# Moving weight loads, ordering the last transfers, spin matmuls and a pipelined MLP in a cached-attention decode kernel

## The chip, the cores and the metric

The kernel runs on one core of one Trainium2 chip. The metric is the device time of one execution in microseconds; the kernel before takes 878.12 us (median of 13 runs, 876.05 to 878.97). Engines are called PE (TensorE), PEld (its weight loads), DVE (VectorE), ACT (ScalarE), POOL (GpSimd) and SP (SyncE, which here only issues DMAs). A profiled execution has a span some 1.8 us shorter than its device time.

## The reference

Two rounds of attention and MLP on a tiny activation (8 rows of 640), with a large cache:

```python
x = x + A(layernorm(x));  x = x + B(layernorm(x))      # and both once more
# A: q = x @ wq (640 x 4096), 32 heads of 128; the last 1024 positions of k_cache, v_cache
#    p = softmax(q k^T / sqrt(128)); o = p v; return o @ wo (4096 x 640)
# B: y = layernorm(x); h = gelu(y @ w1 + b1) (640 x 1728); return h @ w2 + b2
```

Each attention reads 64 MB of K and 64 MB of V in bf16, in 32 chunks of 2 MB each (8 heads of one batch row). Weights: WQ 5.2 MB, WO 5.2 MB, W1 and W2 2.2 MB each.

## The kernel before

Per chunk, DVE makes the scores of 6 heads (48 fused multiply-and-sum instructions), PE those of 2; ACT takes the exps; PE multiplies with V ("PV", 64 one-column matmuls). K has three buffers, V two. K is issued on SP's DMA queue, V on ACT's. WO has no memory of its own: it goes into the K buffers when their last chunk is done.

```python
@block.gpsimd                                  # at the start of the program
def _(g):
    ...
    S_W1.inc(g.dma_start(W1[:, :, :], ...))    # 2.2 MB
    S_W2.inc(g.dma_start(W2[:, 0:FC - 1, :], ...))
    S_W2.inc(g.dma_start(W2[0:F_LAST, FC - 1, :], ...))

@block.scalar
def _(sc):
    S_WQ.inc(sc.dma_start(WQ[:, :, :], ...))   # 5.2 MB; K waits for it
...
# in the attention, on SP, after the last K chunk:
for (c, i, h0, nh) in sorted(woq):             # c: last chunk of K buffer i
    sy.wait_ge(S_QKD.handle, qkd_end[c])       # DVE is done with it
    sy.wait_ge(S_PQ.handle, ...)               # PE is done with it
    S_WO[i].inc(sy.dma_start(WOB[i][:, :, :], A_wo[h0 * Dh:(h0 + nh) * Dh, :]...))
...
# PE at the end of the attention
emit_pv(NCHUNK - 1)                            # waits for exps and for the last V
emit_den(bt0 + B - 1)
...                                            # broadcast of 1/den, OTS on DVE, then
for n0, n1 in [(0, 512), (512, D)]:            # the projection: 32 wide, 32 narrow
    for h in range(H):
        ins = t.matmul(WO_PS[0:8, n0:n1], OTS[:, h * 8:h * 8 + 8], WO(h)[:, n0:n1], ...)
...
# the MLP, each engine by itself over 4 column groups:
#   PE:  W1, all groups      DVE: u, v, z of all groups     ACT: tanh of all groups
#   DVE: h of all groups     PE: transposes, DVE: copies    PE: second projection, all
```

The score loop on DVE, which the change leaves alone, is the line named L347 before and L345 after.

The softmax here doesn't subtract the row's maximum and nothing guards it: scores larger than these inputs give would overflow.

## Time and profile before

| piece of the span (us) | before | what it holds |
|---|---|---|
| start to first score instruction | 35.2 | WQ, first layer norm, first K |
| first score loop | 363.9 | 32 chunks, DVE busy |
| between the loops | 59.6 | last PV, projection, MLP, layer norms, new q |
| second score loop | 364.3 | the same |
| after it | 51.5 | last PV, projection, MLP |
| span | 874.5 | |

The borders are the first and last score instruction of each attention in the timeline. The lines of the profile behind this table stand in the prediction: the chain, the waits of DVE, the chain in order of time and a few stretches. A line of a stretch gives from:to and the length in us, then the busy time and the number of instructions of PE, PEld, DVE, ACT and POOL, then the granted clock (1.00 is full), the DMA share and GB/s. Of the names, KVALL holds the K and V buffers and the WO parts, MPS is the sum of PV, ACC the sum of a projection, OTS what the output projection reads, XT the activation to which a result is added. QROW are the matmuls that make the new q; u, v, z and h are the steps of the MLP's gelu on DVE, hts the copies of its transposes.

### The profile page before, as it was taken

How to read it: one execution, taken by the hardware profiler on the slowest of the kernel's cores; microseconds unless marked ns; L12 is line 12 of the kernel's file. 1: busy time of each engine (PE TensorE's matmuls, PEld its weight loads, DVE VectorE, ACT ScalarE, POOL GpSimd, SP SyncE). 2: the span in 40 equal slices, each digit the busy share in tenths (PEclk: the TensorE clock that was granted, in tenths of full speed). 3: DMA queues.
4: the chain of work that ended last, by engine and by line, in shares of the span. 5: the costliest groups of instructions: out<-in, count | busy, mean ns of one | idle time of the engine just before them, and what ended most of it. 6: DMA issues, size and time to landing. Idle time of an engine off the chain costs nothing.

```text
span 874.5 us, 23472 instructions
## 1 busy us (share of the span) xinstructions
PE 531.3 (61%) x6964; PEld 305.7 (35%) x6964; DVE 732.7 (84%) x6324; ACT 351.8 (40%) x1343; POOL 3.9 (0%) x11
## 2 busy tenths in 40 slices
PE   0866656565666665665458776656565656665456
PEld 0433333333333333342224443333333333333222
DVE  1399999999999999993529999999999999999615
ACT  3444444444434444440335544444444444444121
POOL 1000000000000000000000000000000000000000
PEclk9955555555555555555777555555555555555577
DMA  9999999999999999994706999999999999999800
GB/s 372 381 387 386 385 364 377 365 373 365 372 369 376 379 366 370 368 355 149 288 15 234 359 385 386 386 385 372 370 362 374 360 380 360 378 369 366 282 3 1
DMA packets 143072, 290.16 MB, mean 332 GB/s; under 512 B 2256, under 2 KB 10464, under 8 KB 142304
## 3 DMA queue, kind: packets, MB, share of 16 engines
q1 hardware_dynamic: 74864, 144.72, 45.2%
q10 hardware_dynamic: 67248, 139.50, 43.9%
q0 software_dynamic: 832, 4.44, 1.3%
q8 instruction: 55, 0.90, 0.4%
q14 instruction: 73, 0.60, 0.2%
HBM read 288.64 MB, written 0.01 MB: 330 GB/s over the span
## 4 chain that ended last, share of the span: by engine, by line
DVE 80%; DMA 7%; PE 6%; issue 4%; ACT 2%; DVEq 1%; ACTq 0%
DVE SCRD L347 73%; DVE MLPSCR L347 4%; PE ACC L632 3%; DMA WQ<-in_A_wq_dram 2%; DMA KVALL<-in_A_v_cache_dram 2%; DMA KVALL<-in_A_k_cache_dram 1%; PE ACC L759 1%; DMA KVALL<-in_A_wo_dram 1%; PE P L675 1%; DVE DSUM L318 1%; DVE RDEN L320 1%; DVEq L346 0%; ACT L251 0%; ACT L249 0%; PE MPS L448 0%
## 5 line engine op out<-in xcount | busy, mean ns | idle before, releaser
L347 DVE CUSTOM_DVE_ANT_0 SCRD<-KVALL,QBCB 128x128 bf16<-128x128 bf16 x3072 | 683.6, 287 | 57.9 <-DMA KVALL<-in_A_k_cache_dram 20.9
L347 DVE DVE_READ_ACCUMULATOR2_ANT MLPSCR<- 128x1 f32 x3072 | 250.6, 82 | 0.2
L532 ACT ACTIVATE KTS<-P 128x128 bf16<-128x128 bf16 x512 | 142.1, 278 | 163.8 <-PE P L414 59.0
L520 ACT ACTIVATE QBCB<-P 128x512 bf16<-128x512 f32 x128 | 69.4, 594 | 221.4 <-DVE MLPSCR L347 213.2
L381 PE MATMUL P<-QROWS,UF 8*128 8x512 bf16 x128 | 62.5, 578 | 145.1 <-ACT QBCB L520 143.7
L532 ACT ACTIVATE KTS<-TPS 128x128 bf16<-128x128 bf16 x512 | 139.6, 273 | 2.4
L414 PE MATMUL TPS<-IDENT,KVALL 128*128 128x128 bf16 x512 | 139.9, 273 | 0.0
L414 PE MATMUL P<-IDENT,KVALL 128*128 128x128 bf16 x512 | 138.1, 270 | 0.0
L448 PE MATMUL MPS<-MLPSCR,KVALL 128*128 128x1 bf16 x4096 | 119.2, 165 | 20.3 <-DMA KVALL<-in_A_v_cache_dram 19.4
L424 PE MATMUL P<-QCOL,KTS 128*128 128x1 bf16 x512 | 91.2, 187 | 57.8 <-ACT KTS L532 56.8
L424 PE MATMUL ACC<-QCOL,KTS 128*128 128x1 bf16 x512 | 91.0, 187 | 54.0 <-ACT KTS L532 53.5
L448 PEld LDWEIGHTS MPS<-MLPSCR,KVALL 128*128 128x128 bf16 x4096 | 114.1, 104 | 25.4 <-issue 18.9
L424 PEld LDWEIGHTS P<-QCOL,KTS 128*128 128x128 bf16 x512 | 54.0, 105 | 119.4 <-ACT KTS L532 110.4
L424 PEld LDWEIGHTS ACC<-QCOL,KTS 128*128 128x128 bf16 x512 | 54.0, 105 | 114.6 <-ACT KTS L532 105.2
L381 PEld LDWEIGHTS P<-QROWS,UF 8*128 8x128 bf16 x128 | 12.1, 98 | 172.1 <-issue 149.8
L414 PEld LDWEIGHTS P<-IDENT,KVALL 128*128 128x128 bf16 x512 | 59.4, 116 | 26.9 <-issue 26.9
L414 PEld LDWEIGHTS TPS<-IDENT,KVALL 128*128 128x128 bf16 x512 | 59.8, 117 | 0.0
L367 PE MATMUL P<-WQ,YTS 128*8 128x512 bf16 x80 | 20.8, 422 | 11.0 <-DMA WQ<-in_A_wq_dram 9.6
L632 PE MATMUL ACC<-KVALL,OTS 128*8 128x128 bf16 (+1 forms) x128 | 22.7, 345 | 3.6 <-DMA KVALL<-in_A_wo_dram 2.4
L228 ACT ACTIVATE UF<-XT 8x640 f32<-8x640 f32 x4 | 2.9, 735 | 53.9 <-DVE XT L641 41.3
L551 ACT ACTIVATE MLPSCR<-MLPSCR 128x48 bf16<-128x48 f32 x64 | 15.6, 244 | 16.7 <-DVE MLPSCR L347 16.7
L641 DVE TENSOR_TENSOR XT<-XT,ACC 8x640 f32<-8x640 f32 x2 | 1.6, 808 | 24.0 <-PE ACC L632 24.0
(67 smaller groups left out, 182.7 us busy)
## 6 DMA issues: line engine op xcount, KB each, us to landing
KVALL<-in_A_k_cache_dram SPq DMA_DIRECT2D x64, 2048.0 KB, 17.2
KVALL<-in_A_v_cache_dram ACTq DMA_DIRECT2D x64, 2048.0 KB, 18.2
KVALL<-in_A_wo_dram SPq DMA_DIRECT2D x4, 1920.0 KB, 12.5
WQ<-in_A_wq_dram ACTq DMA_DIRECT2D x1, 5120.0 KB, 21.8
KVALL<-in_A_wo_dram SPq DMA_DIRECT2D x2, 1280.0 KB, 16.4
W<-in_B_w_dram POOLq DMA_DIRECT2D x1, 2160.0 KB, 16.8
W<-in_B_w_dram POOLq DMA_DIRECT2D x1, 2080.0 KB, 23.8
W<-in_B_w_dram POOLq DMA_DIRECT2D x1, 80.0 KB, 23.7
```

The costliest lines, as they stand in the source:

```text
L318: S_DVM.inc(v.tensor_reduce(out=DSUM[:, :], in_=den[0:1, 0:H * J].rearrange("p (h j) -> p h j", j=J), axis=AXX, op=ALU.add))
L320: v.reciprocal(out=RDEN[:, (pb - bt0) * H:(pb - bt0 + 1) * H], in_=DSUM[:, :])
L347: ins = v.tensor_tensor_reduce(out=SCRD[:, slot, :], in0=k_buf[:, hh, j, :], in1=QBCB[gc % 2][:, hh, :], scale=SCALE, scalar=0.0, op0=ALU. ...
L367: ins = t.matmul(QRPS[gq % 2][0:8, 0:QG * Dh], YTS[:, c, :], WQ[:, c, qg * QG * Dh:(qg + 1) * QG * Dh], start=(c == 0), stop=(c == DC - 1))
L381: S_QBM.inc(t.matmul(QPS[qb % 2][:, :], SELB[0:8, b, :], QROWS[0:8, (g * HC + hf * QG) * Dh:(g * HC + (hf + 1) * QG) * Dh], start=True, st ...
L414: S_TP.inc(t.transpose(TPOS[n % 2][:, 0:128], k_buf[:, hh, j, :], IDENT128[:, :]))
L424: S_PQ.inc(t.matmul(SCPS[gc % 2][:, col:col + 1], KTS[n % 2][:, :], QCOL[:, h, b:b + 1], start=True, stop=True))
L448: ins = t.matmul(OTP[:, col:col + 1], v_buf[:, hh, j, :], PB[bt % 2][:, h * J + j:h * J + j + 1], start=(j == 0), stop=(j == J - 1))
L520: S_QEB.inc(sc.activation(QBCB[gc % 2][:, hf * QG:(hf + 1) * QG, :], QPS[qb % 2][:, :].rearrange("p (h d) -> p h d", h=QG), ACTF.Copy))
L532: S_KTE.inc(sc.activation(KTS[n % 2][:, :], TPOS[n % 2][:, 0:128], ACTF.Copy))
L551: S_EXP.inc(sc.activation(PB[bt % 2][:, g * HC * J:(g * HC + hdv) * J], SB[bt % 2][:, g * HC * J:(g * HC + hdv) * J], ACTF.Exp))
L632: ins = t.matmul(WO_PS[0:8, n0:n1], OTS[:, h * 8:h * 8 + 8], WO(h)[:, n0:n1], start=(h == 0), stop=(h == H - 1))
```

## The change

Its intent: use DMA where it idles and keep PE's clock up where DVE does not work. (1) The MLP weights leave the start and follow WO on SP's queue. (2) WO's heads are dealt out in the order in which the K buffers come free, so the projection uses the parts as they arrive (they were already issued in that order), and the second part waits for the last V. (3) "Spin" matmuls, whose results nobody reads, stand before, between and after the real ones. (4) The MLP's four groups are interleaved over the engines. (5) SP issues the first two V chunks of the second attention early.

```diff
-            S_W1.inc(g.dma_start(W1[:, :, :], ...))          # on GpSimd, at the start
-            S_W2.inc(g.dma_start(W2[:, 0:FC - 1, :], ...))
-            S_W2.inc(g.dma_start(W2[0:F_LAST, FC - 1, :], ...))
...
+        def spin(t, dst, n):
+            # matmuls whose result nobody reads: they only keep TensorE's clock up
+            for _ in range(n):
+                t.matmul(dst[0:8, 0:512], IDENT128[:, 0:8], WQ[:, 0, 0:512], start=True, stop=True)
...  # layer norm, all but the first of the program
+                    spin(t, MPS, 10)
+                    t.wait_ge(S_ACM.handle, acm_stat)
+                    spin(t, MPS, 8)
+                    t.wait_ge(S_ACM.handle, acm_sqrt)
+                    spin(t, MPS, 4)
                 t.wait_ge(S_ACM.handle, acm_y)
...                  # transposes of y
+                    spin(t, MPS, 4)
...  # end of the attention, PE
+                t.wait_ge(S_QKD.handle, qkd_end[gc0 + NCHUNK - 1] - 2)
+                spin(t, QPS[0], 9)
                 emit_pv(NCHUNK - 1)
                 emit_den(bt0 + B - 1)
+                spin(t, QPS[0], 3)
...                  # broadcast of 1/den
+                spin(t, QPS[0], 3)
...  # ACT, V loads
+                    if a >= 1 and ci < NVB:
+                        S_VDB[gc % NVB].count += 16
+                        return
...  # SP, K loads
+                    if a >= 1 and ci == NKB - 1:
+                        for ce in range(NVB):
+                            ...                       # V chunk ce of the second attention
...  # SP, WO parts, sorted by their buffer's last chunk
+                    if idx_ == 1:
+                        lastg = gc0 + NCHUNK - 1
+                        sy.wait_ge(S_VDB[lastg % NVB].handle, 16 * (lastg // NVB + 1))
...
                 if a == 0:
+                    S_W1.inc(sy.dma_start(W1[:, :, :], ...))
+                    S_W2.inc(sy.dma_start(W2[:, 0:FC - 1, :], ...))
+                    S_W2.inc(sy.dma_start(W2[0:F_LAST, FC - 1, :], ...))
...  # MLP: after W1 spin(t, MPS, 6), after the first transposes spin(t, MPS, 4), and the order
+            dve_uvz(0); act_tanh(0); dve_uvz(1); act_tanh(1); dve_h(0); pe_T(0)
+            dve_uvz(2); act_tanh(2); dve_hts(0); pe_o2(0); dve_h(1); pe_T(1)
+            dve_uvz(3); act_tanh(3); dve_hts(1); pe_o2(1); dve_h(2); pe_T(2)
+            dve_h(3); pe_T(3); dve_hts(2); pe_o2(2); dve_hts(3); pe_o2(3)
```

(The last four lines are one call per line in the source.) With the new dealing the WO parts also have other sizes: in the first attention the part that goes first has 12 heads instead of 8.

More of the change, by code (lines that the diff above doesn't have):

```diff
@@ L94, in bass_interleave_layers__sliding_block_cached__mixer_channel_mlp__decode_kernel @@
         HPK = KU // D
-        WO_PARTS = []
-        _h0 = 0
-        for _i in range(NKB):
-            _nh = min(HPK, H - _h0)
-            WO_PARTS.append((_i, _h0, _nh))
-            _h0 += _nh
-        assert _h0 == H
-        WOB = [KVALL[:, i * KU:i * KU + nh * D].rearrange("p (k n) -> p k n", k=nh) for (i, h0, nh) in WO_PARTS]
-        def WO(h):
-            for pi, (i, h0, nh) in enumerate(WO_PARTS):
-                if h0 <= h < h0 + nh:
-                    return WOB[pi][:, h - h0, :]
-            raise AssertionError
+        assert HPK * NKB >= H
+        WOB = [KVALL[:, i * KU:i * KU + HPK * D].rearrange("p (k n) -> p k n", k=HPK) for i in range(NKB)]
         QBCB = [T(f"QBCB{i}", [128, HC, Dh], BF16) for i in range(2)]
@@ L204, in _ @@
             S_GD.inc(g.dma_start(XT[0][0:B, :], A_x.rearrange("b s d -> (b s) d")))
-            S_W1.inc(g.dma_start(W1[:, :, :], B_w1.rearrange("(c p) n -> p c n", p=128)))
-            S_W2.inc(g.dma_start(W2[:, 0:FC - 1, :], B_w2[0:(FC - 1) * 128, :].rearrange("(k p) n -> p k n", p=128)))
-            S_W2.inc(g.dma_start(W2[0:F_LAST, FC - 1, :], B_w2[(FC - 1) * 128:F, :]))
         G_SETUP = S_G.count
@@ L220, in bass_interleave_layers__sliding_block_cached__mixer_channel_mlp__decode_kernel, with emit_ln_yt @@
         DVM_IDENT = S_DVM.count
-        def emit_ln_yt(xin, x_ready_waits):
+        def emit_ln_yt(xin, x_ready_waits, warm=False):
             @block.scalar
@@ L267, in _ @@
             def _(t):
+                if warm:
+                    spin(t, MPS, 10)
[3 more added lines that the diff above has]
+                    spin(t, MPS, 4)
                 t.wait_ge(S_ACM.handle, acm_y)
@@ L273, in _ @@
                 S_PEM.inc(ins)
+                if warm:
+                    spin(t, MPS, 4)
             pem_yt = S_PEM.count
@@ L287, in emit_A @@
             a = glob["a"]
-            dvm_yts = emit_ln_yt(xin, x_ready)
+            dvm_yts = emit_ln_yt(xin, x_ready, warm=(a >= 1))
             gc0 = glob["gc"]
@@ L485, in _ @@
                             emit_den(bt0 + (ci - 1) // NG)
+                t.wait_ge(S_QEB.handle, 2 * (gc0 + NCHUNK))
+                t.wait_ge(S_QKD.handle, qkd_end[gc0 + NCHUNK - 1] - 2)
+                spin(t, QPS[0], 9)
                 emit_pv(NCHUNK - 1)
                 emit_den(bt0 + B - 1)
+                spin(t, QPS[0], 3)
                 t.wait_ge(S_RDEN.handle, bt0 + B)
@@ L594, in _ @@
                     assert S_KDB[kbi].count == 16 * (gc // NKB + 1)
-                woq = []
-                for (i, h0, nh) in WO_PARTS:
+                    if a >= 1 and ci == NKB - 1:
+                        for ce in range(NVB):
+                            ge = gc0 + ce
+                            sy.wait_ge(S_PV.handle, ge - NVB + 1)
+                            sy.dma_start(VB[ge % NVB][:, :, :, :], A_v_cache[ce // NG, (ce % NG) * HC:(ce % NG + 1) * HC, W0:W0 + W, :].rearrange("h (p j) d -> p h j d", p=128)).then_inc(S_VDB[ge % NVB].handle, 16)
+                order = sorted(range(NKB), key=lambda i: max(cc for cc in range(gc0, gc0 + NCHUNK) if cc % NKB == i))
+                womap = {}
+                h0 = 0
+                for i in order:
+                    nh = min(HPK, H - h0)
+                    womap[i] = (h0, nh)
+                    h0 += nh
+                assert h0 == H
+                glob["womap"] = womap
+                for idx_, i in enumerate(order):
                     c = max(cc for cc in range(gc0, gc0 + NCHUNK) if cc % NKB == i)
-                    woq.append((c, i, h0, nh))
-                for (c, i, h0, nh) in sorted(woq):
                     sy.wait_ge(S_QKD.handle, qkd_end[c])
                     sy.wait_ge(S_PQ.handle, blk_base[c] + hpe_of(c) * J)
-                    S_WO[i].inc(sy.dma_start(WOB[i][:, :, :], A_wo[h0 * Dh:(h0 + nh) * Dh, :].rearrange("(k p) n -> p k n", p=128)))
+                    if idx_ == 1:
+                        lastg = gc0 + NCHUNK - 1
+                        sy.wait_ge(S_VDB[lastg % NVB].handle, 16 * (lastg // NVB + 1))
+                    hh0, nh = womap[i]
+                    S_WO[i].inc(sy.dma_start(WOB[i][:, 0:nh, :], A_wo[hh0 * Dh:(hh0 + nh) * Dh, :].rearrange("(k p) n -> p k n", p=128)))
                 glob["wo_val"] = [S_WO[i].count for i in range(NKB)]
                 if a == 0:
-                    pass
+                    S_W1.inc(sy.dma_start(W1[:, :, :], B_w1.rearrange("(c p) n -> p c n", p=128)))
+                    S_W2.inc(sy.dma_start(W2[:, 0:FC - 1, :], B_w2[0:(FC - 1) * 128, :].rearrange("(k p) n -> p k n", p=128)))
+                    S_W2.inc(sy.dma_start(W2[0:F_LAST, FC - 1, :], B_w2[(FC - 1) * 128:F, :]))
             @block.vector
@@ L622, in _, with wo_of @@
             def _(t):
+                spin(t, QPS[0], 3)
                 t.wait_ge(S_DVM.handle, dvm_ots)
+                womap = glob["womap"]
+                def wo_of(h):
+                    for i, (hh0, nh) in womap.items():
+                        if hh0 <= h < hh0 + nh:
+                            return i, WOB[i][:, h - hh0, :]
+                    raise AssertionError
                 ins = None
@@ L627, in _ @@
                     for h in range(H):
-                        pi = [k for k, (i, h0, nh) in enumerate(WO_PARTS) if h0 <= h < h0 + nh][0]
+                        pi, wt = wo_of(h)
                         if pi not in waited:
@@ L631, in _ @@
                             waited.add(pi)
-                        ins = t.matmul(WO_PS[0:8, n0:n1], OTS[:, h * 8:h * 8 + 8], WO(h)[:, n0:n1],
+                        ins = t.matmul(WO_PS[0:8, n0:n1], OTS[:, h * 8:h * 8 + 8], wt[:, n0:n1],
                                        start=(h == 0), stop=(h == H - 1))
@@ L651, in emit_B @@
         def emit_B(xin, xout, x_ready):
-            dvm_yts = emit_ln_yt(xin, x_ready)
+            dvm_yts = emit_ln_yt(xin, x_ready, warm=True)
             GCOLS = [(0, 512), (512, 1024), (1024, 1536), (1536, F)]
+            NGRP = len(GCOLS)
             @block.vector
@@ L670, in _, with dve_uvz @@
                     ins = None
-                    n0 = g0
-                    while n0 < g1:
-                        n1 = min(n0 + 512, g1, ((n0 // 512) + 1) * 512)
-                        for c in range(DC):
-                            ins = t.matmul(HP[0:8, n0:n1], YTS[:, c, :], W1[:, c, n0:n1], start=(c == 0), stop=(c == DC - 1))
-                        n0 = n1
+                    for c in range(DC):
+                        ins = t.matmul(HP[0:8, g0:g1], YTS[:, c, :], W1[:, c, g0:g1], start=(c == 0), stop=(c == DC - 1))
                     S_PEM.inc(ins)
                     pem_hp[gi] = S_PEM.count
+                spin(t, MPS, 6)
             dvm_z = {}
-            @block.vector
-            def _(v):
-                v.wait_ge(WA_B[0].handle, WA_B[1])
-                for gi, (g0, g1) in enumerate(GCOLS):
+            acm_t = {}
+            dvm_h = {}
+            pem_ht = {}
+            dvm_hts = {}
+            pem_o2 = {}
+            def dve_uvz(gi):
+                g0, g1 = GCOLS[gi]
+                @block.vector
+                def _(v):
                     v.wait_ge(S_PEM.handle, pem_hp[gi])
-                    if gi > 0:
-                        v.wait_ge(S_DVM.handle, S_DVM.count)
+                    v.wait_ge(WA_B[0].handle, WA_B[1])
+                    v.wait_ge(S_DVM.handle, S_DVM.count)
                     S_DVM.inc(v.tensor_tensor(UB[0:B, g0:g1], HP[0:B, g0:g1], B1[0:B, g0:g1], ALU.add))
@@ L695, in _, with act_tanh @@
                     dvm_z[gi] = S_DVM.count
-            acm_t = {}
-            @block.scalar
-            def _(sc):
-                for gi, (g0, g1) in enumerate(GCOLS):
+            def act_tanh(gi):
+                g0, g1 = GCOLS[gi]
+                @block.scalar
+                def _(sc):
                     sc.wait_ge(S_DVM.handle, dvm_z[gi])
@@ L703, in _, with dve_h @@
                     acm_t[gi] = S_ACM.count
-            dvm_h = {}
-            @block.vector
-            def _(v):
-                for gi, (g0, g1) in enumerate(GCOLS):
+            def dve_h(gi):
+                g0, g1 = GCOLS[gi]
+                @block.vector
+                def _(v):
                     v.wait_ge(S_ACM.handle, acm_t[gi])
@@ L714, in _, with pe_T @@
                     dvm_h[gi] = S_DVM.count
-            pem_ht = {}
-            NGRP = len(GCOLS)
-            exp_hts = {gi: dvm_h[NGRP - 1] + gi + 1 for gi in range(NGRP)}
-            @block.tensor
-            def _(t):
-                for gi, (g0, g1) in enumerate(GCOLS):
+            def pe_T(gi):
+                g0, g1 = GCOLS[gi]
+                @block.tensor
+                def _(t):
                     t.wait_ge(S_DVM.handle, dvm_h[gi])
                     if gi >= 2:
-                        t.wait_ge(S_DVM.handle, exp_hts[gi - 2])
+                        t.wait_ge(S_DVM.handle, dvm_hts[gi - 2])
                     ins = None
@@ L732, in _, with dve_hts @@
                     pem_ht[gi] = S_PEM.count
-            dvm_hts = {}
-            @block.vector
-            def _(v):
-                for gi, (g0, g1) in enumerate(GCOLS):
+                    spin(t, MPS, [4, 0, 0, 0][gi])
+            def dve_hts(gi):
+                g0, g1 = GCOLS[gi]
+                @block.vector
+                def _(v):
                     v.wait_ge(S_PEM.handle, pem_ht[gi])
@@ L747, in _, with pe_o2 @@
                     dvm_hts[gi] = S_DVM.count
-                    assert dvm_hts[gi] == exp_hts[gi]
-            @block.tensor
-            def _(t):
-                t.wait_ge(WA_W2[0].handle, WA_W2[1])
-                ins = None
-                for gi, (g0, g1) in enumerate(GCOLS):
+            def pe_o2(gi):
+                g0, g1 = GCOLS[gi]
+                @block.tensor
+                def _(t):
+                    if gi == 0:
+                        t.wait_ge(WA_W2[0].handle, WA_W2[1])
                     t.wait_ge(S_DVM.handle, dvm_hts[gi])
+                    ins = None
                     for k in range(g0 // 128, (g1 + 127) // 128):
@@ L760, in _ @@
                                            start=(k == 0), stop=(k == FC - 1))
-                S_PEM.inc(ins)
-            pem_o2 = S_PEM.count
+                    S_PEM.inc(ins)
+                    pem_o2[gi] = S_PEM.count
+                    pass
+            dve_uvz(0)
+            act_tanh(0)
+            dve_uvz(1)
+            act_tanh(1)
+            dve_h(0)
+            pe_T(0)
+            dve_uvz(2)
+            act_tanh(2)
+            dve_hts(0)
+            pe_o2(0)
+            dve_h(1)
+            pe_T(1)
+            dve_uvz(3)
+            act_tanh(3)
+            dve_hts(1)
+            pe_o2(1)
+            dve_h(2)
+            pe_T(2)
+            dve_h(3)
+            pe_T(3)
+            dve_hts(2)
+            pe_o2(2)
+            dve_hts(3)
+            pe_o2(3)
             @block.vector
             def _(v):
-                v.wait_ge(S_PEM.handle, pem_o2)
+                v.wait_ge(S_PEM.handle, pem_o2[NGRP - 1])
                 v.wait_ge(S_DVM.handle, dvm_xb)
```

## The prediction

> **What bounds the kernel now.** I read the page's chain that ended last first, then the waits of VectorE (DVE), then the chain in order of time, then the stretches where DVE is not the one that works.
>
> The page's chain that ended last, by engine:
>
> ```profile
> DVE 80%; DMA 7%; PE 6%; issue 4%; ACT 2%; DVEq 1%; ACTq 0%
> ```
>
> The waits of DVE (us in total, times, longest):
>
> ```profile
> DVE XT L641 <- PE ACC L632: 24.0, 2, 12.6
> DVE SCRD L347 <- DMA KVALL<-in_A_k_cache_dram: 20.9, 1, 20.9
> ...
> DVE XT L768 <- PE ACC L759: 10.6, 2, 5.3
> ...
> DVE SCRD L347 <- DVE MLPSCR L347: 8.8, 49, 0.5
> ...
> DVE SCRD L347 <- ACT QBCB L520: 4.5, 14, 0.3
> ```
>
> Inside its score loop (L347) DVE waits for K once, before the first chunk, and after that only 8.8 + 4.5 us in all. In the timeline the loop runs from 35.20 to 399.07 us in the first attention and from 458.71 to 823.0 in the second: 364 us each, 11.37 per chunk of 2 MB of K and 2 MB of V. Nothing in the diff touches the loop. The other 874.5 - 728 = 146.5 us are three pieces: 35.2 before the first loop, 59.6 between the loops, 51.5 after the second. All that can be won is there. The chain in order of time (start, length, what) shows what holds them:
>
> ```profile
> 0.74 21.81 DMA WQ<-in_A_wq_dram
> 22.57 12.45 DMA KVALL<-in_A_k_cache_dram
> ...
> 384.26 16.56 DMA KVALL<-in_A_v_cache_dram
> 400.96 1.84 PE MPS L448 x64
> ...
> 406.44 11.36 PE ACC L632 x64
> ...
> 439.14 5.53 PE ACC L759 x28
> ...
> 823.02 9.94 DMA KVALL<-in_A_wo_dram
> 833.10 11.36 PE ACC L632 x64
> ```
>
> And stretches of time (last three columns: granted PE clock, DMA share, GB/s):
>
> ```profile
> 396.00:400.00 4.00, 0.00 (x0) 0.00 (x0) 3.12 (x30) 0.24 (x1) 0.00 (x0) 0.50 0.22 76
> 408.10:411.50 3.40, 3.40 (x9) 1.02 (x8) 0.00 (x0) 0.00 (x0) 0.00 (x0) 0.50 0.02 5
> 412.00:415.40 3.40, 3.40 (x17) 1.34 (x16) 0.00 (x0) 0.00 (x0) 0.00 (x0) 1.00 0.00 0
> 820.00:824.00 4.00, 0.00 (x0) 0.00 (x0) 2.96 (x28) 0.24 (x1) 0.00 (x0) 0.50 0.09 33
> ```
>
> The same output matmuls come 9 in 3.4 us at clock 0.50 and 17 at 1.00. While the last V is waited for, DMA moves 33 to 76 GB/s instead of 370: by the packet records, one lagging engine is still working while fifteen are done.
>
> **What the Trainium skill says.** "TensorE: Matmul & The Clock Gate", Part 1: TensorE runs at half clock by default and is let go after some 3.4 us of sustained work; an idle window of that length takes it back. The trace agrees: the output matmuls start at 406.44 and speed up at 411.5; the clock is half again in the middle of the next layer norm. The page says little on partly busy windows; in this trace a window with the QROW matmuls over about 82% of it was enough, one about 25% busy lost the clock. "DMA: Bandwidth & Descriptors", "Queues, rings and completion order": each of the 16 engines takes packets in turn from the queues that have work, so a second queue's transfer halves the first. The trace agrees: while WQ was alone its queue moved about 410 GB/s, with the MLP weights beside it some 220.
>
> **Part 1: the MLP weights leave the start.** WQ is 5.24 MB and lands at 22.57. By then queue 0 has also moved about 2.9 MB of the MLP weights; at the 413 GB/s of that stretch this is 7 us, so WQ should land near 15.6. K is issued when WQ lands. Its first chunk took 12.45 us, because some 1.4 MB of the MLP weights and then V were served with it; the fastest K load of the whole run, with the queues empty, took 7.5. So K0 lands near 23.3. The broadcast q that DVE also needs was ready 5.6 us after WQ (28.18 against 22.57), hence at 21.2: K decides. Gain 35.2 - 23.4 = 11.8. The second chunk then follows a shorter head start and may come late by half a microsecond: **-11.3**. The loop behind it needs 4.19 MB per 11.37 us, 369 GB/s, where DMA gives 385, so it moves forward as a block.
>
> The 4.4 MB come back behind the first attention's WO on the SP queue: 11.4 us at 385 GB/s. W1 is needed some 23 us after the last V lands. In the queue stand two WO parts (3.3 MB), then W1 (2.2 MB): about 2 + 8.5 + 5.7 = 16 us. Hidden.
>
> **Part 2: last V before WO.** The second WO part now waits for the last V. The lagging engine shared its time between V and WO for most of the final microseconds. With V alone it should finish near 398.7 (before 400.8) and 823.3 (before 826.3). PV also needs the last exp, at 399.43 and about 823.3. Gain **-1.4** in the first attention, **-2.8** in the second. In the second, the WO parts were also waited for after OTS (831.9 to 833.1, 1.2 us). The new order uses them as they arrive, but its last part lands some 11 to 12 us after V, just when wanted: **-1.2 + 0.5**.
>
> **Part 3: spin for the clock.** Output projection: 12 of 32 wide matmuls ran at 427 ns instead of 215: 12 x 0.212 = 2.5 us if it starts warm. PE is idle up to PV, the 9 spins start some 3.4 us before DVE ends, last 9 x 0.427 = 3.8, and PV with its small columns may not count as busy: I take **-2.0** per attention, and **+0.2** for spins that stand before the broadcast matmul. Layer norm takes 8.4 us from projection to W1; the 10, 8, 4 and 4 warm spins fit in its waits (2.15 in 2.55, 1.7 in 3.0, 0.9 in 1.1). In the second attention QROW is warm from its start: 6.5 x 0.212 = **-1.3**.
>
> **Part 4: the MLP in a pipeline.** Before: W1 starts at 426.20, the last add at 444.70, 18.5 us. Of that, 2.4 to the first group, 10.9 of DVE in a row (three groups of 2.0 and one of 1.15; then h 2.4; then hts 1.3), and 5.3 waiting for all of L759. The new order, worked out group by group with warm matmuls: first group at 1.35; u, v, z of groups 0 and 1 to 5.35; h0 to 6.0; group 2 to 8.0; hts0 to 8.35, L759 for group 0 beside it; h1 9.0; group 3 10.15; hts1 10.5; h2 and h3 11.7; the transposes of groups 2 and 3 behind L759 for group 1 at 12.3; hts2 and hts3 to 13.0; L759 for groups 2 and 3 to 14.6; add at 14.8. DVE's work is the same, what vanishes is most of L759 at the end. Full gain 3.7. With a cold PE the same walk gives 19.0, no gain: L759 for a group is then 2.2 us and stands in the way of the next transposes. The spins (6, then 4) are there for this; I take **-3.2** each.
>
> **Part 5: K and V prefetch for the second attention.** K is still issued after the output projection, now behind W1 and W2 on the same queue, then the first two V. The DMA has nothing to do from 436 to 456 before, so 10.5 MB end before DVE starts. DVE had no K or V wait there: **0**.
>
> **Sum.** Start -11.3. Between the loops: -1.4 - 2.0 + 0.2 - 3.2 - 1.3 = -7.7. After the second loop: -2.8 - 1.2 + 0.5 - 2.0 + 0.2 - 3.2 = -8.5. Total -27.5, and 877.3 - 27.5 = 849.8; as the spin counts look tuned on the chip I lean to the warm side and say 849.
>
> **Rivals.** (a) TensorE does not warm where it should. For: the window is free-running, PV columns are short, and 60% busy in the score loop stayed at 0.50 throughout. Against: the output matmuls alone warm in 5 us. Then 2 x (2.0 + 3.2) + 1.3 = 11.7 us are lost, and spins of 427 ns outlast the layer norm's waits by 1 to 2 us each: 861 to 865. (b) Everything is warm and V is on time: -2.5, -3.7 and no late chunk: 846, and 842 if the start also gives 2 more. (c) The moved DMA collides: W1 or W2 late, or K0 of the second attention held behind them. For: some 20 MB are now queued in a row. Against: the idle 20 us of DMA. Should V and WO drag on by 10 us, the result would be 858. (d) The start is hidden anyway, because the loop then waits for DMA: it asks 369 of 385 GB/s, so I rate it low; it would make 856.
>
> **Range and chances.** The start alone (-11.3) and the ordering of V (-4) need no warm clock: about 860 without the rest, at the 2% line of 859.8. With even half of the rest it is under. Range 842 to 857; faster 0.95, within 2% 0.05, slower 0.
>
> **What would show it.** First L347 near 23.5 us; loops still about 364 us each; WO and W1 matmuls at clock 1.00 from their first; 64 output matmuls in 9 us instead of 11.4; from W1 to the last add 15 us; from the end of the second loop to the end 43 instead of 51.5; between the loops 52 instead of 59.6. Wrong if the loops lengthen, if the clock row shows 0.50 in the MLP, or if W1 matmuls wait for DMA.

## The result, and the profile after

The changed kernel takes 852.86 us (median of 8 runs, 851.48 to 856.76); the ratio to the kernel before is 0.9719, with a 95% interval of 0.9705 to 0.9734. Ratios are the mean time of one kernel's fast runs over that of the other's of the same rounds, so not quite the ratio of the medians. The prediction was 849, range 842 to 857.

| piece (us) | before | after | change | predicted |
|---|---|---|---|---|
| start | 35.2 | 23.9 | -11.3 | -11.3 |
| first loop | 363.9 | 363.9 | 0 | 0 |
| between: loop's end to last PV | 1.82 | 2.79 | +1.0 | -1.4 |
| last PV to projection's start | 5.47 | 5.62 | +0.15 | +0.2 |
| projection to add | 11.38 | 10.74 | -0.6 | -2.0 |
| W1 to last add (MLP) | 18.50 | 14.21 | -4.3 | -3.2 |
| last add to next loop | 14.01 | 12.70 | -1.3 | -1.3 |
| second loop | 364.3 | 364.3 | 0 | 0 |
| after it: to last PV | 3.48 | 0.68 | -2.8 | -2.8 |
| last PV to projection's start | 6.63 | 5.78 | -0.85 | -0.5 |
| projection to add | 11.39 | 10.53 | -0.9 | -2.0 |
| W1 to last add (MLP) | 18.50 | 14.21 | -4.3 | -3.2 |
| span | 874.5 | 849.2 | -25.3 | -27.5 |

The rows are differences of start times in the timeline; the layer norm between add and W1 is 8.4 us in both and left out, as is the end after the last add, 3.1 us in both. (The -0.5 predicted for the second attention's way from last PV to projection is the prediction's -1.2 + 0.5 + 0.2.) The profiled execution of the changed kernel, 851.04 us, is its fastest, and that of the kernel before, 876.28, is near its fastest.

The chain that ended last, by engine, is quite another one now:

```profile
DMA 42%; DVE 34%; PE 15%; ACT 6%; issue 3%; ACTq 0%; DVEq 0%; SPq 0%
```

This is no change of what bounds the loop: the loop is as long as it was, to 0.02 us. It says that the last PV was released by a V transfer, and that this transfer leads back through the whole loop: PV n frees the buffer for V n+2. The waits of PE for V (us in total, times, longest) show the same; before, then after:

```profile
PE MPS L448 <- DMA KVALL<-in_A_v_cache_dram: 19.4, 6, 7.8
```

```profile
PE MPS L446 <- DMA KVALL<-in_A_v_cache_dram: 34.5, 31, 2.8
```

Half of all PVs now wait for V. In the loop that costs nothing, as DVE does not wait for PV; at its end it does. The chain in order of time after (start, length, what):

```profile
0.76 15.39 DMA WQ<-in_A_wq_dram
...
376.27 14.23 DMA KVALL<-in_A_v_cache_dram
391.03 12.20 DMA KVALL<-in_A_wo_dram
403.27 3.69 PE ACC L661 x40
...
427.64 1.90 PE ACC L792 x12
...
807.62 12.15 DMA KVALL<-in_A_wo_dram
819.82 3.69 PE ACC L661 x40
```

WQ lands 6.4 us earlier. The last V lands at 390.5, 2.7 us after the loop's end at 387.84, and the WO parts behind it follow in the chain, though PE waits for them only 0.4 us in all. Of the MLP's second projection only 12 matmuls, 1.90 us, stand at the end, where there were 28 and 5.53. Two stretches of the changed kernel around its last V (columns as in the prediction):

```profile
378.00:383.00 5.00, 3.06 (x25) 1.60 (x24) 4.89 (x45) 3.09 (x15) 0.00 (x0) 0.50 1.03 390
384.00:390.00 6.00, 5.19 (x59) 2.23 (x56) 3.67 (x34) 0.24 (x1) 0.00 (x0) 0.58 0.08 28
```

390 GB/s are 24 for each of 16 engines. From 384 to 390 DMA moves 28 in all: one engine. The landing records of this V agree: 15 of its 16 increments come from 383.6 to 384.2, the last at 390.5. And the stretches of the projection:

```profile
396.30:399.20 2.90, 2.90 (x9) 0.81 (x8) 0.00 (x0) 0.00 (x0) 0.00 (x0) 0.50 1.07 367
399.30:402.00 2.70, 2.70 (x14) 1.05 (x13) 0.00 (x0) 0.00 (x0) 0.00 (x0) 1.00 1.06 375
```

The projection still starts at half clock, in spite of the spins ahead of it. The MLP does not; before, then after:

```profile
426.20:432.00 5.80, 5.80 (x14) 1.75 (x15) 3.73 (x8) 0.63 (x1) 0.00 (x0) 0.50 1.05 387
432.00:439.00 7.00, 1.79 (x21) 1.14 (x19) 6.26 (x29) 1.62 (x3) 0.00 (x0) 0.74 0.52 191
439.00:444.70 5.70, 5.66 (x30) 2.48 (x29) 0.40 (x7) 0.00 (x0) 0.00 (x0) 0.72 0.00 0
```

```profile
415.30:419.00 3.70, 3.65 (x20) 1.72 (x21) 2.86 (x6) 0.44 (x1) 0.00 (x0) 1.00 1.05 388
419.00:425.50 6.50, 4.10 (x29) 1.57 (x26) 5.86 (x23) 1.49 (x4) 0.00 (x0) 1.00 1.05 387
425.50:429.50 4.00, 3.44 (x27) 1.60 (x28) 1.67 (x13) 0.31 (x1) 0.00 (x0) 1.00 1.05 384
```

So three questions are open: why is the last V of the first attention later and not earlier; what does each of order and clock give to the MLP; and was the V prefetch really worth nothing?

### The profile page after: what moved, and what is told of

The parts are those of the page before. It is cut to its first block, busy times and chain, and to the rows that moved or that the text cites. A ratio compares the mean times of both kernels' runs of the same rounds, so it can differ in the third digit from the quotient of the medians.

```text
span 849.2 us, 23730 instructions
## 1 busy us (share of the span) xinstructions
PE 556.5 (66%) x7092; PEld 313.0 (37%) x7092; DVE 732.6 (86%) x6324; ACT 353.9 (42%) x1343; POOL 1.3 (0%) x8
## 4 chain that ended last, share of the span: by engine, by line
DMA 42%; DVE 34%; PE 15%; ACT 6%; issue 3%; ACTq 0%; DVEq 0%; SPq 0%
DMA KVALL<-in_A_v_cache_dram 38%; DVE SCRD L345 29%; PE MPS L446 5%; DMA KVALL<-in_A_wo_dram 3%; ACT KTS L537 3%; PE P L365 2%; DMA WQ<-in_A_wq_dram 2%; DVE MLPSCR L345 1%; PE P L412 1%; PE P L422 1%; PE P L379 1%; PE P L471 1%; PE ACC L422 1%; PE ACC L661 1%; PE ACC L792 1%
## 5 line engine op out<-in xcount | busy, mean ns | idle before, releaser
L446 PE MATMUL MPS<-MLPSCR,KVALL 128*128 128x1 bf16 x4096 | 118.6, 165 | 35.1 <-DMA KVALL<-in_A_v_cache_dram 34.5
L188 PE MATMUL MPS<-WQ,IDENT 128*8 128x512 bf16 x98 | 23.8, 379 | 4.7 <-ACT STAT L241 3.4
L661 PE MATMUL ACC<-KVALL,OTS 128*8 128x128 bf16 (+1 forms) x128 | 20.8, 324 | 0.4 <-DMA KVALL<-in_A_wo_dram 0.4
## 6 DMA issues: line engine op xcount, KB each, us to landing
KVALL<-in_A_wo_dram SPq DMA_DIRECT2D x4, 1920.0 KB, 14.8
```

The source lines that it names most:

```text
L188: t.matmul(dst[0:8, 0:512], IDENT128[:, 0:8], WQ[:, 0, 0:512], start=True, stop=True)
L446: ins = t.matmul(OTP[:, col:col + 1], v_buf[:, hh, j, :], PB[bt % 2][:, h * J + j:h * J + j + 1], start=(j == 0), stop=(j == J - 1))
L661: ins = t.matmul(WO_PS[0:8, n0:n1], OTS[:, h * 8:h * 8 + 8], wt[:, n0:n1], start=(h == 0), stop=(h == H - 1))
```

## The experiments

Eleven runs, all with correct results. In each, "+PV" is the time from the end of a score loop to the start of the last PV of that attention (first, second).

**1. MLP weights at the start again.** Everything else of the change kept.

```diff
+            S_W1.inc(g.dma_start(W1[:, :, :], ...))    # GpSimd, start; and both W2
-                    S_W1.inc(sy.dma_start(W1[:, :, :], ...))    # SP; and both W2
```

> The changed kernel with one part undone: W1 and W2 are loaded at the start again, on GpSimd's queue. Theory (pieces outside the score loops add up): WQ lands near 22.6 us instead of 16.2, the first score instruction comes near 35.2 instead of 23.9, nothing else moves: 852.9 + 11.3 = 864. Rival (the start is hidden, since the loop waits for DMA anyway, or the weights in mid-kernel cost as much as they freed at the start): 853 to 857.

Measured: 861.89 us (ratio 0.9825, 0.9797 to 0.9852), 9.0 more than the changed kernel. In its profile the first score instruction comes at 35.05, as expected, but the last PV of the first attention stands at +0.40 instead of +2.79. The start is not hidden: it is worth 11.1 us at the first score instruction. But 2.4 of these are given back at the end of the first loop. I had not expected that; the next two runs ask why.

**2. DVE held back, DMA not.** The first score instruction waits for the second K chunk too.

```diff
                             v.wait_ge(S_KDB[kbi].handle, 16 * (gc // NKB + 1))
+                            if gc == 0:
+                                v.wait_ge(S_KDB[1].handle, 16)
```

> The changed kernel, but the first score instruction waits for the second K chunk as well, so that it starts at 34.2 instead of 23.9 us while DMA starts as early as before. What it tells apart: in the changed kernel the last PV of the first attention starts 2.8 us after the loop's end, and 26 of its 32 PV wait for V; with the MLP weights at the start it was 0.4 us and hardly a wait. Theory (the DMA has a shorter head start over the score loop, and one nearly saturated DMA engine carries that debt through the loop): with the head start back, no V waits in the loop, last PV at +0.4 to +0.8, time 852.9 + 10.3 - 2.3 = 861. Rival (it comes from where the MLP weights or WO stand, not from the head start): last PV still at +2.8, time 863.2.

Measured: 861.59 us (0.9812, 0.9783 to 0.9841); first score instruction at 35.5; +PV 0.34 in the first attention. The waits of PE for V:

```profile
PE MPS L448 <- DMA KVALL<-in_A_v_cache_dram: 5.6, 6, 2.2
```

34.5 us in 31 waits became 5.6 in 6, with the MLP weights where the change put them. It is the head start. Why the loop does not win it back is not shown. By mean rates it could: of some 385 GB/s it asks for 369, and the other 16 would move 5.8 MB in 364 us, while 11.3 us of head start are 4.3 MB (an estimate from these figures). My reading is that the one engine that lags has less to spare than the mean.

**3. WO not held for V.**

```diff
-                    if idx_ == 1:
+                    if idx_ == NKB:                    # never
```

> The changed kernel without the wait of the second WO part for the last V. Theory (one lagging DMA engine serves V and WO in turn, so the wait lets V land sooner): the last PV starts 5.8 us after the first loop's end instead of 2.8 and 3.9 after the second's instead of 0.7; the projection ends 2.7 and 3 us later: +5.7, about 858.5. Rival (with the wait, 15 engines idle for 7 us and WO comes late; without it WO is there when PV ends, which makes up for it): within 1 us of 852.9.

Measured: 859.10 us (0.9786, 0.9771 to 0.9800). +PV is 6.05 and 4.21; expected were 5.8 and 3.9. The wait is worth 6 us: two queues take turns on the lagging engine. By the packet records a 2 KB packet of the last V starts there every 134 to 149 ns while WO stands beside it (390.9 to 393.0 us), and every 80 to 86 ns in the changed kernel once V is alone (from 386.9 us), so V keeps somewhat over half of its rate.

**4. All of WO held for V.**

```diff
-                    if idx_ == 1:
+                    if idx_ == 0:
```

> The changed kernel with the wait for the last V moved from the second to the first WO part. Theory (the lagging engine spends about 5 us on the first WO part, 0.12 MB at 24 GB/s, while V waits): the last V lands before the last exp in both attentions, last PV at +0.5 us; all of WO lands 16 us after V, earlier than now, as the other engines no longer stand idle between: the projection ends 17.3 instead of 19.2 us after the first loop and 15.2 instead of 17.0 after the second: -3.7, about 849. Rival (the lag is V's own, so V is no earlier and all of WO is 6 us later): +6, about 859.

Measured: 852.51 us (0.9714, 0.9687 to 0.9741), the same as the changed kernel. The mechanism was right: +PV is 0.34 in both attentions. The gain is not there: WO lands 18.5 us after V and not 16 (404.2 against 385.7), 15.8 after the first loop's end, and the projection waits for it three times, 3.1 us in all:

```profile
PE ACC L661 <- DMA KVALL<-in_A_wo_dram: 3.1, 3, 2.1
```

In this profile it also lost the clock again in the middle, so that projection and waits took 14.7 us in the first attention. What V gained, WO lost.

**5. No V prefetch.** ACT issues the second attention's first two V chunks itself, as before.

```diff
-                    if a >= 1 and ci < NVB:
+                    if a >= 9 and ci < NVB:            # never
-                    if a >= 1 and ci == NKB - 1:
+                    if a >= 9 and ci == NKB - 1:
```

> The changed kernel with the first two V chunks of the second attention issued by ScalarE again, at the start of that attention. Prediction's term (DVE had no V wait there): 0, so 852.9, last PV of the second attention still at +0.7. Rival (without the prefetch V runs late all through the second loop, as it does in the first): last PV at +2.8, about 855.

Measured: 855.47 us (0.9745, 0.9730 to 0.9759), 2.6 more. The prediction's term for the prefetch, 0, was wrong. V runs late through both loops, and +PV of the second attention is 3.98 instead of 0.68. The waits of PE for V:

```profile
PE MPS L446 <- DMA KVALL<-in_A_v_cache_dram: 78.3, 55, 2.5
```

Together with run 3: with prefetch but without the wait of WO, +PV of the second attention was 4.21; with the wait but without prefetch 3.98; with neither, in the kernel before (which differs in more than these two), 3.48; with both 0.68. Each alone gives nothing there.

**6. No spins.**

```diff
-            for _ in range(n):
+            for _ in range(0):
```

> The changed kernel with no spin matmuls at all, everything else kept. Theory (the pipeline in the MLP needs the warm clock): from the first W1 matmul to the last add near 19 us instead of 14.2, twice; QROW 1.3 slower; output projection 0.6 to 0.9 slower, twice: +12, about 865. Rival (the pipeline alone brings the gain, and PE warms by itself): MLP 15 to 16 us, in all +3 to +5, 856 to 858.

Measured: 862.77 us (0.9840, 0.9813 to 0.9867). From W1 to the last add it takes 18.84 and 18.78 us, about the 18.50 of the old order. The interleaved order alone is worth nothing. Projection to add takes 10.93 and 10.70 us, hardly more than with spins (10.74 and 10.53): those before the projection do next to nothing. The stretches of its first MLP:

```profile
415.80:420.00 4.20, 4.20 (x10) 1.23 (x11) 2.44 (x5) 0.00 (x0) 0.00 (x0) 0.50 1.05 386
420.00:424.40 4.40, 2.38 (x15) 1.05 (x13) 3.79 (x10) 1.26 (x2) 0.00 (x0) 0.89 1.05 387
424.40:434.60 10.20, 8.60 (x38) 3.26 (x38) 4.18 (x25) 0.99 (x2) 0.00 (x0) 0.50 1.05 387
```

W1 warms the clock when it is nearly over, and the next gaps take it away again; the interleaved second projection runs cold.

**7. Old order in the MLP, spins kept.**

```diff
-            dve_uvz(0) ... pe_o2(3)                    # interleaved, as in the change
+            for gi in range(NGRP): dve_uvz(gi); act_tanh(gi)
+            for gi in range(NGRP): dve_h(gi)
+            pe_T(0); pe_T(1); dve_hts(0); pe_T(2); dve_hts(1); pe_T(3); dve_hts(2); dve_hts(3)
+            for gi in range(NGRP): pe_o2(gi)
```

> The changed kernel with the MLP's groups in the old order on all engines (all uvz, then all h, then the transposes, then all of the second projection), spins kept. Theory (clock first, order second): with warm matmuls W1 saves 1.1 and the second projection 1.7 of the old 18.5 us, so 15.8 from W1 to the last add instead of 14.2, twice: +3.2, about 856. Rival (the order is what saved the 4.3 us of each MLP): near 18 us, +7.5, about 860.

Measured: 860.25 us (0.9797, 0.9780 to 0.9813), MLP 19.07 and 18.27 us. The number is the rival's, and my theory, that warm matmuls alone give most of it, was wrong as tested: they were not warm.

```profile
416.40:420.00 3.60, 3.58 (x20) 1.65 (x21) 2.76 (x6) 0.38 (x1) 0.00 (x0) 1.00 1.05 387
420.00:424.00 4.00, 1.53 (x9) 0.51 (x6) 3.53 (x9) 1.21 (x3) 0.00 (x0) 1.00 1.05 386
424.00:428.60 4.60, 2.54 (x18) 1.00 (x18) 3.94 (x24) 0.66 (x2) 0.00 (x0) 0.50 1.05 389
428.60:435.40 6.80, 6.80 (x30) 2.86 (x31) 0.22 (x2) 0.00 (x0) 0.00 (x0) 0.58 1.05 386
```

In the old order PE has 4.1 us without work while DVE makes u, v, z of the other groups. At 424 the clock falls, and the 28 matmuls of the second projection take 6.8 us at its end.

**8. Old order, with that gap filled.** 23 spins after W1 instead of 6.

```diff
-                spin(t, MPS, 6)
+                spin(t, MPS, 23)                       # on top of run 7
```

> The kernel with the MLP's groups in the old order, with 23 instead of 6 spins after W1, which fill the 4.1 us that PE waited there for the first h. Theory (old order lost its gain because PE idled 4 us in mid-MLP and the clock fell): clock 1.00 to the end of the MLP, from W1 to the last add 16 us instead of 18.3 to 19.1, time 852.9 + 2 x 1.8 = 856.5. Rival (the order itself is what counts): MLP 18 us, 860.

Measured: 855.09 us (0.9743, 0.9728 to 0.9758), MLP 15.85 and 15.84 us, clock 1.00 throughout. The stretch in which run 7 lost it:

```profile
420.00:424.00 4.00, 4.00 (x20) 1.58 (x19) 3.49 (x10) 1.26 (x2) 0.00 (x0) 1.00 1.05 386
```

So the order is worth 1.6 us per MLP once PE is warm (15.85 against 14.21), and the warm clock 2.65 (18.50 against 15.85). Runs 6, 7 and 8 together: the interleaving's larger merit is that it leaves PE no long gap.

**9 to 11. A version that does better.** If the harm is that WO and V stand in two queues, they can stand in one: the three WO parts are issued by ACT, behind the last V in ACT's queue. Nothing then waits for V, and 15 engines go straight on to WO. W1 and W2 wait for the last WO part. Run 11 adds four spins inside the last PV. The changed kernel ran again beside them.

```diff
                     if 1 <= ci and ci + 1 < NCHUNK:
                         emit_vdma(ci + 1)              # ACT
+                    if ci - 1 >= NCHUNK - NKB:
+                        emit_wo_dma(ci - 1)            # waits for DVE and PE on that K buffer, then WO
...
-                    S_WO[i].inc(sy.dma_start(...))     # SP, with the wait for V before the second
+                    sy.wait_ge(S_WO[order[-1]].handle, glob["wo_val"][order[-1]])   # before W1
...
+                        if ci == NCHUNK - 1 and hh % 2 == 1:    # run 11 only
+                            spin(t, QPS[0], 1)
```

> The changed kernel once more, on the same chip and in the same rounds as the two that follow. All theories: 852.9, ratio to before 0.972, last PV at +2.8 us after the first loop and +0.7 after the second.

> The changed kernel with the three WO parts issued on ScalarE's DMA queue, behind the last V, each as soon as its K buffer is free, with no wait for V at all; W1 and W2 wait for the last WO part. Theory (what hurts is that WO and V stand in two queues and the lagging engine takes them in turn; in one queue V goes first and the 15 other engines go straight on to WO): last PV at +0.4 us in both attentions, as when all WO waited for V, and all of WO landed by +11.5 instead of +15.4 and +13.3; projection ends at +16.1 instead of +19.2 and +17.0: -4.0, about 849. Rival (V is no earlier, or ScalarE's DMA issues hold up the score loop): loop longer or PV at +2.8, 853 to 856.

> The same, with one spin after every two heads of the last PV, four in all. Theory (PV with its one-column matmuls does not count as work for the clock, which is why the projection starts at half clock in spite of the spins before it): 0.9 us more in PV, 7 wide matmuls at 215 instead of 427 ns, -0.6 per attention, about 848. Rival (the window needs more than that): +1 to +2, 850 to 851.

Measured on one chip: the changed kernel 852.88 us (0.9724, 0.9711 to 0.9737), WO on ACT's queue 848.92 us (0.9674, 0.9659 to 0.9689), with the four spins 850.82 us (0.9720, 0.9695 to 0.9744). WO on ACT's queue is 4.0 us better, as expected, its interval clear of the changed kernel's. +PV is 0.54 and 0.34, WO lands at +11.9 and +10.1, and the projection ends at +16.4 and +16.3. The hole in DMA is gone; its stretches around the last V:

```profile
383.00:386.00 3.00, 2.98 (x69) 2.23 (x70) 2.86 (x27) 0.45 (x4) 0.00 (x0) 0.50 1.06 371
386.00:389.00 3.00, 3.00 (x8) 0.69 (x6) 2.48 (x24) 0.24 (x1) 0.00 (x0) 0.50 1.07 361
389.00:394.00 5.00, 5.00 (x73) 2.76 (x73) 1.00 (x3) 0.00 (x0) 0.00 (x0) 0.50 1.07 363
```

The spins inside PV made the way to the projection 1.5 and 2.2 us longer (PV to its start 7.3 and 7.5 us instead of 5.8 and 5.3). In the first attention the projection still started at half clock and took as long as without them (10.08 and 10.02 us); in the second the clock rose 1.4 us after its start instead of 3.6 (9.59 us against 10.67), which does not pay for the delay. That theory failed. One caution from these profiles: in the changed kernel run again, the clock fell once in the second MLP, which then took 15.27 us; the same kernel had 14.21 in its first profile. It also fell in one or both MLPs of the profiles of runs 1, 2 (both), 3, 5 and 10: in 7 of the 18 MLPs that were profiled with spins and the new order, which then took 15.3 to 16.4 us. So the MLP's spins are enough more often than not, but not every time, and a difference of 1 or 2 us between two runs can come from this alone. It is probably part of the 851 to 857 us that the changed kernel's runs spread over (the slowest, 856.76 us, has the lowest mean clock, 0.566 against 0.572 in the fastest).

## Why the prediction was right, point by point

**The bound and the three pieces: right.** The loops kept their length to 0.02 us, and everything was won outside.

**Part 1, the start: right at its place, -11.3 of -11.3, but not free.** Rival (d), that the start is hidden, named the right danger at the wrong spot: the loop did not wait for DMA. But "so it moves forward as a block" was the step that failed. DVE moved by 11.3 us and V by less. Run 1 puts the net worth at 9.0 us, run 2 shows that the lost head start is the cause. Rival (c), a collision of the moved weights, did not happen.

**Part 2, V before WO: right in the second attention (-2.8), wrong in sign in the first (+1.0 for -1.4).** The term itself was sized well: with the head start back, in run 2, +PV was 0.34, which is 1.5 less than before. What the sum lacked is the debt of part 1, together with the first WO part, which the change leaves beside the last V. With that part behind V too (runs 4 and 10), the head start is as short and PE still waits for V 21.4 and 38.3 us in all, but +PV is 0.34 and 0.54. So either cure is enough: the head start, or V before all of WO.

**Part 3, the clock: right for QROW (-1.3), too high for the projection.** I put 2.0 us per attention on it; 0.6 and 0.9 came, and run 6 shows that most of these come without spins too (10.93 and 10.70 us against 11.4 before). The step that failed is that the spins let the projection start warm; the clock rose only 3.0 and 2.6 us after its start. The prediction's own doubt, that "PV with its small columns may not count as busy", fits: the clock fell at the end of the last PV. But it isn't the whole cause. From 392.39 to 395.81 us, after PV, PE is listed busy all the time with spins and the broadcast matmul, and the clock did not rise, and run 11's spins inside PV did not make the first projection warm. This stays open.

**Part 4, the MLP: right, -4.3 for -3.2.** The walk through the groups gave 14.8 us warm and 19.0 cold; measured were 14.21 and 18.8. I discounted it for a clock that held. As the prediction's walk had it, the order needs the clock: order without spins 18.8, the same spins without the order 18.3 to 19.1, neither 18.5, both 14.2. Without the order the clock takes more spins (run 8), and then gives 2.65 of the 4.3. The prediction's sign of being wrong, 0.50 in the MLP, did not show in this profile, but it did in others (see the caution above).

**Part 5, the prefetch: wrong, 2.6 us and not 0.** "DVE had no K or V wait there" was true and not to the point: the V debt is seen in PE's waits, and it is paid at the last PV.

The sum, -27.5 for -25.3 in the span, was near because the first attention's V and the projection (4.9 us too high) stand against the MLPs (2.2 too low); that is luck. (It starts from 877.3 us; the median measured is 878.12.) The prefetch error is hidden within the -2.8 of part 2.

## What to carry to other kernels

When a loop uses nearly all of the DMA rate, moving its start earlier than its data leaves a debt that no wait of the bound engine shows: look at the waits of the engine whose result ends the loop. Where one transfer is wanted before another for speed, try them in one DMA queue before guarding one with a wait for the other; here it was worth 4.0 us. (This is about which is served first. Whoever uses the data still waits for its semaphore, as all runs here do.) Plan spins and reordering for PE's clock together: each alone, as they stand in the change, gave nothing here, and the clock of the stretches shows where the gap is that still has to be filled.

## What the Trainium skill lacked or had wrong

- "DMA: Bandwidth & Descriptors", "Latency and other measured facts", tells of two engines that are usually slower and calls this specific to the software queue. In the changed kernel that queue carries 0.02 MB, and one engine still ends the last V 6.3 us after the fifteenth (390.5 against 384.2). The records name neither the engine nor the cause. They do show that it serves more than this data: in the profiles of runs 1, 2 and 5, when it alone still works on V, its packets stop for an 8 KB instruction fetch of queue q14 (in run 5 from 808.91 to 809.22 us, with a V packet ending at 808.92 and the next starting at 809.22). In the changed kernel that queue moves 0.59 MB. Whether this is why it lags stays open.
- The same page, "Queues, rings and completion order": that queues take turns on each engine is confirmed (in the changed kernel's packet records WO and V packets alternate from 385.55 to 386.85 us; +PV is 6.05 us with WO in a second queue, 0.54 with WO behind V in one). It lacks what follows for ordering: a wait for the completion of a transfer idles the engines that are done, here down to 28 GB/s for 6 us.
- "TensorE: Matmul & The Clock Gate", Part 1, speaks of idle and busy windows. It lacks how much work holds the clock: it held with PE listed busy 4.10 of 6.5 us, and fell after 1.53 of 4.0.
- The same part lacks that busy time in a trace is not what the clock gate sees. In the changed kernel the clock was 1.00 from 389.0 and fell at 392.4; in between PE is listed busy for more than half of the time, with the end of the spins and the last PV of 64 one-column matmuls. A stretch of the same length in the MLP, mostly spins of 512 columns, is listed just as busy, and the clock held:

```profile
389.00:392.40 3.40, 1.96 (x66) 1.77 (x66) 0.00 (x0) 0.00 (x0) 0.00 (x0) 1.00 0.20 29
419.70:423.11 3.41, 1.97 (x12) 0.55 (x10) 3.07 (x9) 0.63 (x1) 0.00 (x0) 1.00 1.05 387
```

Both are 58%. (All clock changes of this trace are whole multiples of 3.41 us apart, and both stretches begin and end on that grid.)
